# Layer 2's weight conversion in another order, with the squares' remainder put back by three points

## The chip, the cores and the metric

The kernel runs on one NeuronCore of one Trainium2 chip. The metric is the device time of one execution in microseconds (us). Before the change the median of three runs is 893.32 us (893.29 to 895.34).

Engines are named as the profile names them: PE multiplies matrices and PEld loads its weights, DVE (VectorE) and ACT (ScalarE) work element by element, POOL is GpSimd, SP issues most transfers (DMAs). Each engine takes its instructions in the order in which they were written down.

## The reference

```python
scores = scale * np.matmul(q, k.transpose(0, 1, 3, 2))      # masked local and strided, softmax, times v
...
x = np.ascontiguousarray(attn_out.transpose(0, 2, 1, 3)).reshape(B * S, H * D)
h = x @ w_in                        # layer 1: 2304 x 512 by 512 x 2048
r = np.maximum(h, 0.0)
g = r * r
x = g @ w_out                       # 2048 x 512
h = np.maximum(x @ w_in2, 0.0)      # layer 2, same shapes
return h * h @ w_out2
```

Attention over 4 batches and 8 heads gives 2304 tokens of 512 numbers. Two layers follow, each a product to 2048 columns, a ReLU, a square and a product back to 512. The weights of both layers arrive as 64-bit floating point numbers.

## The kernel before, in words

**Numbers.** Matmuls run on FP32R operands, so each 32-bit operand is split into a high part (a copy rounded to FP32R, made by ACT) and a low part (value minus high, made by DVE). A product is three matmuls: high by high, low by high, high by low.

**Steps.** Layer 1 works on five blocks of tokens: 512, 512, 512, 256, 512 wide. A step `s` is one block and 128 of the 2048 columns (256 of them in the 256-wide block). The main loop issues for step `s` first `mm1(s + 1)`, 12 matmuls of 512 columns (or 24 of 256) into a PSUM bank, and then `mm2(s)`, as many into the block's four banks `ps_y`. Steps 0 to 47 are blocks 0 to 2, steps 48 to 55 the 256-wide block, steps 56 to 71 the last block. Steps 72 to 79 are the first block of layer 2, 256 wide (`narrow`); from then on layer 2 uses seven products per 2 by 2 blocks in place of eight (`seven`), for which sums and differences of the weights are needed.

**Between mm1 and mm2** (`mm1`, lines 1012 to 1022). While weights are converted, ACT makes `r`, the ReLU of the bank (L1012), `sq`, its square (L1017), and `gh`, the rounded copy (L1018). DVE makes `gl = sq - gh` (L1022), the remainder. `mm2` reads `gh` in its first eight matmuls and `gl` in the last four. `r` and `sq` have one buffer each, `gh` and `gl` two.

**Points.** Each step has eight places between matmuls at which other work may be issued: three in `mm1`, one behind it, three in `mm2`, one behind it (`point`, L1553). Once attention has been issued, about step 46, each point adds 0.6 (`w_out`) or 0.68 (`w_in`) to a credit (`PACES`), and for each whole credit `conv2_by` issues one unit of the list `conv2`.

**The conversion of layer 2's weights** (`conv2`, L433). There are 32 pieces of 128 x 512: 16 of `w_out`, then 16 of `w_in`, taken in pairs. For a piece, `sign2` puts the sign into the lower words (DVE, L242 and L246), `range2` shifts the exponent of the upper words (ACT, L263), `whole2` joins both to 32-bit values (DVE, L268), `high2` copies the high part (ACT, L368) and `rest2` takes the low part (DVE, L375). For a pair, `sums_1` and `sums_2` make four sums and differences (DVE, L386), `high_s` their high parts (ACT, L420) and `sums_3` their low parts (DVE, L386, 128x1024). Before the change, a pair's nine units run from its signs to `sums_3`, and the next pair begins behind it.

**Transfers.** For a pair of `w_out`, `rest2` of the second piece stores 1 MB to `w_mem` (L378) and `sums_3` another 1 MB (L426), both from a fixed place in `xall` that the next pair's `high2` and `high_s` overwrite. `whole2` and `sums_3` then load a raw piece of 512 KB into the buffer that they have just read (L225). Pieces of `w_in` are loaded one per step from step 56 on. All of these stand in SP's queue.

**Ends of blocks.** In a block's last step `mm2` copies each finished bank to a tile `o` (ACT, L1067) and stores it to `y_dram` (L1069), in the last two blocks of layer 1 from ACT's own queue. The tiles are `tag="pt"`, which has two buffers, so the third copy waits until the first store has landed. In steps 60 to 69 the first rows come back as `y_in` (`load_y`, `tag="s"`, also two buffers) and are split (`split_y`, L955 and L956).

Of the kernel before, what the change touches and what calls it, by code (L numbers as in the profile page):

```python
# [9 lines left out]
F32 = mybir.dt.float32  # L10
# [4 lines left out]
ALU = mybir.AluOpType  # L15
AX = mybir.AxisListType

P = 128
# [146 lines left out]
def r32(ap):  # L165
    return ap.bitcast(F32)
# [3 lines left out]
def tile_attention_then_two_mlps(  # L170
# [259 lines left out]
            load2("out")  # L430


    conv2 = []  # L433
    for i in range(0, half2 + 2, 2):
        if i:
            conv2.append([(sums_3, i - 2)])
        if i < half2:
            conv2 += [
                [(sign2, i)],
                [(sign2, i + 1), (range2, i)],  # L440
                [(whole2, i), (range2, i + 1)],
                [(whole2, i + 1), (high2, i)],
                [(sums_1, i), (high2, i + 1)],
                [(sums_2, i)],
                [(rest2, i), (high_s, i)],
                [(rest2, i + 1)],
            ]

    def conv2_by(n):
        while n and n_conv2[0] < len(conv2):  # L450
# [526 lines left out]
    def mm1(s, point):  # L977

        if s >= len(steps):
            return  # L980
        k, f = steps[s]
        ne = tiles_of(k)
        n = TB // ne
        x_hi, x_lo = block_x(k)
        if s != 1 and n_att[0] >= att_end[-1]:
            ps = ps_a.tile([P, TB], F32, tag="a", name="ps_h")
        elif s != 1:
            ps = ps_h.tile([P, TB], F32, tag="h", name="ps_h")
        else:
            ps = ps_a.tile([P, TB], F32, tag="a", name="ps_h")  # L990
        for c in range(KC):
            for e in range(ne):
                w = ready2(f + e) if k == NB else ready(("in", 0, f + e))
                for i, (a, x) in enumerate(((0, x_hi), (0, x_lo), (1, x_hi))):

                    last = c == KC - 1 and i == 2 and e == ne - 1
                    product(
                        ps[:, e * n:(e + 1) * n],
                        lhsT=w[:, c // 2, a, c % 2 * P:(c % 2 + 1) * P] if k == NB
                        else w[:, a, c * P:(c + 1) * P],  # L1000
                        rhs=x[:, c] if k == NB else x[:, c, x_at(n):x_at(n) + n],
                        start=c == 0 and e == 0 and i == 0,
                        stop=last,
                        halves=last and k == NB - 1 and f == 0,
                    )
                    one_small()
            if c < KC - 1:
                point()
        g0 = 48 if ne > 1 and blocks[k][0] == 0 else 0
        r = gpool.tile([P, TB], F32, tag="r", name="r", bufs=1)  # L1010
        sq = gpool.tile([P, TB], F32, tag="sq", name="sq", bufs=1)
        nc.scalar.activation(out=r, in_=ps, func=AF.Relu, scale=W_BACK)  # L1012
        h = gpool.tile([P, TB + P], F32R, tag="gh", name="gh", bufs=2)[:, g0:g0 + TB]
        lo = gpool.tile([P, 3 * HALF], F32R, tag="gl", name="gl", bufs=2)[:, g0:g0 + TB]
        if 0 < n_load[0] - n_part[0] or 0 < n_conv2[0] < len(conv2):

            nc.scalar.activation(out=sq, in_=r, func=AF.Square)  # L1017
            nc.scalar.activation(out=h, in_=sq, func=AF.Copy)  # L1018
        else:
            nc.scalar.activation(out=h, in_=r, func=AF.Square)  # L1020
            nc.vector.tensor_tensor(out=sq, in0=r, in1=r, op=ALU.mult)  # L1021
        nc.vector.tensor_tensor(out=lo, in0=sq, in1=r32(h), op=ALU.subtract)  # L1022
        gh[s], gl[s] = h, lo

    def mm2(s, point):

        k, f = steps[s]
        layer, j = blocks[k]
        t0, n = BLOCKS[layer][j]
        ne = tiles_of(k)  # L1030
        ws = [ready(("out", layer, f + e)) for e in range(ne)]
        h, lo = gh.pop(s), gl.pop(s)

        if f == 0:
            ys[k] = [ps_y.tile([P, 512], F32, tag=f"y{c}", name="ps_y") for c in range(KC)]
        end = f + ne == NF

        def narrow_at(s):
            return s < len(steps) and tiles_of(steps[s][0]) > 1

        todo = []
        for c, y in enumerate(ys[k]):
            cols = slice(c * P, (c + 1) * P)
            for i, (a, gp) in enumerate(((0, h), (1, h), (0, lo))):
                for e, w in enumerate(ws):
                    g0 = e * n
                    todo.append((i, c, y[:, :n], w[:, a, cols], gp[:, g0:g0 + n]))
        if not end:

            todo.sort(key=lambda t: t[0] == 2)  # L1050
        places = [-(-len(todo) * (i + 1) // 4) - 1 for i in range(3)]
        last = {t[1]: m for m, t in enumerate(todo)}
        seen = set()
        for m, (i, c, y, lhsT, rhs) in enumerate(todo):
            product(
                y,
                lhsT=lhsT,
                rhs=rhs,
                start=f == 0 and c not in seen,
                stop=end and m == last[c],  # L1060
                halves=m == len(todo) - 1 and rhs.shape[-1] == TB and narrow_at(s + 2),
            )
            seen.add(c)
            one_small()
            if end and m == last[c]:
                t = apool.tile([P, 512], F32, tag="pt", name="o")[:, :n]
                nc.scalar.activation(out=t, in_=y, func=AF.Copy, scale=W_BACK)  # L1067
                queue = nc.scalar if j >= NB - 2 else nc.sync
                queue.dma_start(out=y_dram[:, c, t0:t0 + n], in_=t)  # L1069
            if m in places:  # L1070
                point()
# [450 lines left out]
    with tc.manual_schedule():  # L1522

        zeros = gpool.tile([P, TB], F32, tag="sq", name="zeros", bufs=1)[:, :P]
        nc.vector.memset(zeros, 0.0)
        ps = ps_h.tile([P, TB], F32, tag="h", name="ps_w")[:, :P]
        for _ in range(N_WARM):
            nc.tensor.matmul(ps, lhsT=zeros, rhs=zeros, start=True, stop=True)
        warm += [ps, zeros]
        for n in range(5):  # L1530
            if n < 3:
                load_qk()
            if n == 0:
                nc.sync.dma_start(out=cst, in_=consts)
            load_v()
        rounds = 0
        while n_att[0] < att_end[0]:
            att_to(min(n_att[0] + len(ALONE), att_end[0]))
            load_ahead(START_LOAD[rounds])
            conv_by(START_CONV[rounds])  # L1540
            rounds += 1
        def nothing():
            pass

        mm1(0, nothing)
        for s in range(len(steps)):
            k, f = steps[s]
            layer, j = blocks[k]
            n_pt = [0]
            load_ahead(4)  # L1550
            for fn, k2, c in y_at.get(s, ()):
                fn(k2, c)

            def point(s=s, layer=layer, j=j, f=f):
                n_pt[0] += 1
                at = N_PT * s + n_pt[0]
                for b, (p0, p1) in enumerate(spans):
                    if at > p0:
                        lo, hi = att_end[b], att_end[b + 1]
                        if b == 0 and at < LATE * N_PT:  # L1560
                            hi = lo + (hi - lo) * EARLY // 100
                            p1 = LATE * N_PT
                        elif b == 0:
                            lo += (hi - lo) * EARLY // 100
                            p0 = LATE * N_PT
                        att_to(min(hi, lo + -(-(hi - lo) * (at - p0) // (p1 - p0))))
                if n_part[0] < half1:
                    conv_by(1)
                elif n_att[0] >= att_end[-1] and n_conv2[0] < len(conv2):
                    if not n_load2["out"]:  # L1570
                        for _ in range(4):
                            load2("out")
                    credit[0] += PACES[conv2[n_conv2[0]][0][1] >= NF]
                    while credit[0] >= 1.0:
                        conv2_by(1)
                        credit[0] -= 1.0

            if k == NB:
                narrow(s, point)
                continue  # L1580
            if s + 1 == first_2:
                narrow_w(0)
            mm1(s + 1, point)
            point()
            mm2(s, point)
            point()
            if k == NB - 1:
                load2("in")
        seven()
# [37 lines left out]
```

## Time and profile before, and how to read it

| what | value |
|---|---|
| median of three runs | 893.32 us |
| the profiled execution's own time | 893.98 us |
| its span in the trace | 892.2 us |
| PE busy | 858.4 us, 96% |
| PEld busy | 772.6 us, 87% |
| DVE busy | 684.3 us, 77% |
| ACT busy | 528.5 us, 59% |

A trace row gives the start and length of an instruction, its engine, its line, what it writes and reads, and, in brackets, how long the engine stood idle before it and what released it. A view of waits sums these by pair of engine and releaser. A view by windows gives busy time per stretch, the granted clock of PE, the busy share of the DMA engines and their GB/s. Merged rows ("x12") are equal instructions in a row. Ends of matmuls are modelled.

### The profile page before, as it was taken

Reading aid. Unit: us, or ns where it says so; the run is one execution under the profiler, and the core shown is the slowest. Engines: PE = TensorE matmul, PEld = TensorE weight load, DVE = VectorE, ACT = ScalarE, POOL = GpSimd, SP = SyncE. Lnnn points to the kernel's source line nnn. Section 1 sums busy time; section 2 is a strip of 40 time slices with the busy share of each in tenths; the row PEclk is TensorE's granted clock in tenths of the full one; section 3 lists DMA queues with packets and bytes.
Section 4 is the critical chain, followed back from the end, with each engine's and each line's share of the span. In section 5 each row is a group of like instructions: output and inputs, shape, how many; then the busy total and the mean of one; then the engine's idle time right before and its main releaser. Section 6 shows DMA issues by size and latency. Waiting matters only on the chain. (4 is left out here: it accounts for less than half of the span.)

```text
span 892.2 us, 16045 instructions
## 1 busy us (share of the span) xinstructions
PE 858.4 (96%) x5719; PEld 772.6 (87%) x5719; DVE 684.3 (77%) x1742; ACT 528.5 (59%) x1216; POOL 17.7 (2%) x15
## 2 busy tenths in 40 slices
PE   8899999999999999998988888999999999999998
PEld 8788888888788888897866667899999999999997
DVE  5899884588867775587577767578888888888876
ACT  6977774576656664565655565455555555555542
POOL 0700000000000000000000000000000000000000
PEclk9999999999999999999999999999999999999999
DMA  8956520232322221487884365467667667766664
GB/s 275 331 190 196 186 75 26 97 90 71 87 84 73 65 64 54 164 301 291 279 290 129 118 206 192 145 201 230 194 195 259 201 189 220 255 192 198 223 190 130
DMA packets 81247, 155.21 MB, mean 174 GB/s; under 512 B 7440, under 2 KB 36240, under 8 KB 78096
## 3 DMA queue, kind: packets, MB, share of 16 engines
q1 hardware_dynamic: 80016, 152.62, 52.6%
q10 hardware_dynamic: 1152, 1.57, 0.5%
q8 instruction: 45, 0.74, 0.3%
q14 instruction: 34, 0.28, 0.1%
HBM read 127.95 MB, written 26.21 MB: 173 GB/s over the span
## 5 line engine op out<-in xcount | busy, mean ns | idle before, releaser
L969 PE MATMUL ps_h<-xall,w 128*128 128x512 f32 (+1 forms) x1153 | 247.9, 358 | 0.0
L969 PEld LDWEIGHTS ps_h<-xall,w 128*128 128x128 f32 x1153 | 185.8, 189 | 26.3
L969 PE MATMUL ps_y<-gh,w 128*128 128x512 f32 (+1 forms) x640 | 159.7, 379 | 18.5 <-ACT gh L1018 13.6
L969 PEld LDWEIGHTS ps_y<-gh,w 128*128 128x128 f32 x640 | 107.5, 189 | 40.9 <-ACT gh L1018 17.8
L1256 PE MATMUL ps_m<-xall,s 128*128 128x256 f32 x768 | 104.8, 279 | 0.6 <-DVE u L1091 0.6
L1022 DVE TENSOR_TENSOR gl<-sq,gh 128x512 fp32r<-128x512 f32 x80 | 55.3, 691 | 55.5 <-ACT gh L1018 50.5
L1256 PEld LDWEIGHTS ps_m<-xall,s 128*128 128x128 f32 x768 | 95.5, 188 | 1.8 <-DVE u L1091 1.1
L1283 PE MATMUL ps_y<-w,bh 128*128 128x256 f32 x496 | 91.8, 278 | 0.0
L969 PE MATMUL ps_y<-gl,w 128*128 128x512 f32 (+1 forms) x324 | 84.9, 373 | 0.0
L1256 PE MATMUL ps_m<-xall,w 128*128 128x256 f32 x576 | 83.3, 280 | 0.0
L1012 ACT ACTIVATE r<-ps_h 128x512 f32<-128x512 f32 x80 | 47.2, 590 | 56.6 <-PE ps_h L969 47.7
L1283 PEld LDWEIGHTS ps_y<-w,bh 128*128 128x128 f32 x496 | 75.3, 188 | 0.0
L1256 PEld LDWEIGHTS ps_m<-xall,w 128*128 128x128 f32 x576 | 74.2, 188 | 0.4 <-ACT u L1336 0.4
L1283 PE MATMUL ps_y<-w,ah 128*128 128x256 f32 x372 | 70.0, 278 | 0.0
L1283 PE MATMUL ps_y<-w,bl 128*128 128x256 f32 x248 | 68.8, 277 | 0.0
L969 PEld LDWEIGHTS ps_y<-gl,w 128*128 128x128 f32 x324 | 56.3, 190 | 10.4 <-DVE gl L1022 0.9
L1021 DVE TENSOR_TENSOR sq<-r 128x512 f32<-128x512 f32 x38 | 26.3, 691 | 48.8 <-ACT r L1012 48.8
L1091 DVE SCALAR_TENSOR_TENSOR u<-ps_m,u 128x256 f32<-128x256 f32 x96 | 40.5, 421 | 26.4 <-PE ps_m L1256 26.2
L1283 PEld LDWEIGHTS ps_y<-w,ah 128*128 128x128 f32 x372 | 56.7, 189 | 0.0
L1081 ACT ACTIVATE ah<-c 128x256 fp32r<-128x256 f32 x33 | 13.7, 417 | 71.8 <-DVE c L1265 71.7
L674 ACT ACTIVATE s<-s,m 96x128 f32<-96x128 f32 (+2 forms) x88 | 34.3, 390 | 34.2 <-DVE m L558 33.6
L263 ACT ACTIVATE raw<-raw 128x512 f32<-128x512 f32 x49 | 33.1, 676 | 32.8 <-DVE raw L246 32.4
(121 smaller groups left out, 1526.5 us busy)
## 6 DMA issues: line engine op xcount, KB each, us to landing
w<-w_mem SPq DMA_DIRECT2D x221, 256.0 KB, 2.8
raw<-moe_w_in_d SPq DMA_DIRECT2D x32, 512.0 KB, 5.5
w_mem<-xall SPq DMA_DIRECT2D x16, 1024.0 KB, 5.2
raw<-moe_w_out_d SPq DMA_DIRECT2D x24, 512.0 KB, 5.3
xall<-w_mem SPq DMA_DIRECT2D x8, 1024.0 KB, 5.1
qk<-loc_qk_d SPq DMA_DIRECT2D x12, 416.0 KB, 3.1
out_d<-o SPq DMA_DIRECT2D x17, 256.0 KB, 2.4
others<-moe_w_out_d SPq DMA_DIRECT2D x8, 512.0 KB, 6.0
```

The lines of the kernel that those rows point to most:

```text
L263: nc.scalar.activation(out=upper, in_=upper, func=AF.Copy, scale=2.0 ** (W_EXP // 8 - 112))
L674: nc.scalar.activation(out=blk, in_=blk, func=AF.Exp, scale=-1.0, bias=m[:nq, j:j + 1], accum_out=dens[i][:nq, j:j + 1],)
L969: nc.tensor.matmul(y[:, c:c + w], lhsT=lhsT, rhs=rhs[:, c:c + w], start=start and c == 0, stop=stop and c + w == n,)
L1012: nc.scalar.activation(out=r, in_=ps, func=AF.Relu, scale=W_BACK)
L1021: nc.vector.tensor_tensor(out=sq, in0=r, in1=r, op=ALU.mult)
L1022: nc.vector.tensor_tensor(out=lo, in0=sq, in1=r32(h), op=ALU.subtract)
L1081: nc.scalar.activation(out=hi, in_=src, func=AF.Copy)
L1091: nc.vector.scalar_tensor_tensor(out=dst, in0=src, scalar=sign * W_BACK, in1=to, op0=ALU.mult, op1=ALU.add)
L1256: nc.tensor.matmul(ps[:, half * HT:(half + 1) * HT], lhsT=w[:, j * P:(j + 1) * P], rhs=x[:, j], start=half == 0 and j == 0 and m == 0, sto ...
L1283: nc.tensor.matmul(banks[name][:, t * HALF:(t + 1) * HALF], lhsT=g[:, rows], rhs=w, start=first and t == 0 and m == 0, stop=end and t == 1 ...
```

## The change

The list `conv2` begins with the first pair's signs and ranges. Each pair then has its own `whole2`, `sums_1`, `sums_2`, `rest2` and `sums_3`, with the next pair's two signs and two ranges between. The remainder of the squares (L1022, now L1025) is no longer issued behind `gh`, but at the third point from there, while `conv2` has begun and not ended; `point` calls `remainders` after `conv2_by`. The tiles `o` of the last two blocks of layer 1 take `tag="s"` for odd banks and `"pt"` for even ones, so four buffers in all.

```diff
-    conv2 = []
-    for i in range(0, half2 + 2, 2):
-        if i:
-            conv2.append([(sums_3, i - 2)])
-        if i < half2:
-            conv2 += [
-                [(sign2, i)],
-                [(sign2, i + 1), (range2, i)],
-                [(whole2, i), (range2, i + 1)],
-                [(whole2, i + 1), (high2, i)],
-                [(sums_1, i), (high2, i + 1)],
-                [(sums_2, i)],
-                [(rest2, i), (high_s, i)],
-                [(rest2, i + 1)],
-            ]
+    conv2 = [[(sign2, 0)], [(sign2, 1)], [(range2, 0)], [(range2, 1)]]
+    for i in range(0, half2, 2):
+        n = i + 2 if i + 2 < half2 else None
+        conv2 += [
+            [(whole2, i)],
+            [(whole2, i + 1)],
+            [(sums_1, i), (high2, i)],
+            [(sums_2, i), (high2, i + 1)],
+            [(sign2, n)],
+            [(rest2, i), (high_s, i)],
+            [(sign2, n and n + 1), (range2, n)],
+            [(rest2, i + 1)],
+            [(sums_3, i), (range2, n and n + 1)],
+        ]
...
-        nc.vector.tensor_tensor(out=lo, in0=sq, in1=r32(h), op=ALU.subtract)
+        def remainder():
+            nc.vector.tensor_tensor(out=lo, in0=sq, in1=r32(h), op=ALU.subtract)
+        if 0 < n_conv2[0] < len(conv2):
+            behind.append([3, remainder])
+        else:
+            remainder()
...
+    def remainders(all_of_them=False):
+        for one in list(behind):
+            one[0] -= 1
+            if one[0] == 0 or all_of_them:
+                one[1]()
+                behind.remove(one)
...
-                t = apool.tile([P, 512], F32, tag="pt", name="o")[:, :n]
+                t = tile_of("s" if c % 2 and j >= NB - 2 else "pt")[:, :n]
...
-                elif n_att[0] >= att_end[-1] and n_conv2[0] < len(conv2):
+                elif n_att[0] >= att_end[-1] and (behind or n_conv2[0] < len(conv2)):
...
                     while credit[0] >= 1.0:
                         conv2_by(1)
                         credit[0] -= 1.0
+                    remainders()
```

PE's order is the same in both kernels. On DVE, in the last block of layer 1 while `w_in` is converted, the rows from one remainder (`gl`) to the next were, in the kernel before (`raw` are the 64-bit words, `s` the sums, `w` the weights' parts):

```order
1014 L1022 TENSOR_TENSOR gl<-sq,gh 128x512
1015 L242 TENSOR_SCALAR raw<-raw 128x512
1016 L246 SCALAR_TENSOR_TENSOR raw<-raw 128x512
1017 L268 SCALAR_TENSOR_TENSOR val<-raw 128x512 x2
1018 L386 TENSOR_TENSOR s<-val 128x256 x2
1019 L386 TENSOR_TENSOR s<-s,val 128x256
1020 L386 TENSOR_TENSOR s<-val,s 128x256
1021 L375 TENSOR_TENSOR w<-val,w 128x2x256
1022 L1022 TENSOR_TENSOR gl<-sq,gh 128x512
1023 L375 TENSOR_TENSOR w<-val,w 128x2x256
1024 L386 TENSOR_TENSOR s<-s 128x1024
```

and in the changed kernel, in the same block:

```order
1023 L1025 TENSOR_TENSOR gl<-sq,gh 128x512
1024 L386 TENSOR_TENSOR s<-s 128x1024
1025 L268 SCALAR_TENSOR_TENSOR val<-raw 128x512 x2
1026 L386 TENSOR_TENSOR s<-val 128x256 x2
1027 L386 TENSOR_TENSOR s<-s,val 128x256
1028 L386 TENSOR_TENSOR s<-val,s 128x256
1029 L242 TENSOR_SCALAR raw<-raw 128x512
1030 L246 SCALAR_TENSOR_TENSOR raw<-raw 128x512
1031 L1025 TENSOR_TENSOR gl<-sq,gh 128x512
1032 L375 TENSOR_TENSOR w<-val,w 128x2x256
1033 L958 TENSOR_TENSOR xall<-y_in,xall 128x256
```

A sign of the next pair now stands between a pair's sums and its first `rest2` (L375), and the remainder stands behind that sign. On ACT, in the same stretch, the rows ahead of one `r` were, before (`w` and `s` are the high parts of weights and of sums):

```order
549 L263 ACTIVATE raw<-raw 128x512 x2
550 L368 ACTIVATE w<-val 128x2x256 x2
551 L420 ACTIVATE s<-s 128x1024
552 L1012 ACTIVATE r<-ps_h 128x512
553 L1017 ACTIVATE sq<-r 128x512
554 L1018 ACTIVATE gh<-sq 128x512
```

and in the changed kernel:

```order
551 L263 ACTIVATE raw<-raw 128x512 x2
552 L1014 ACTIVATE r<-ps_h 128x512
553 L1019 ACTIVATE sq<-r 128x512
554 L1020 ACTIVATE gh<-sq 128x512
555 L368 ACTIVATE w<-val 128x2x256 x2
556 L420 ACTIVATE s<-s 128x1024
557 L957 ACTIVATE xall<-y_in 128x256
558 L263 ACTIVATE raw<-raw 128x512
559 L1014 ACTIVATE r<-ps_h 128x512
```

Ranges (L263) of one pair and high parts (L368, L420) of the same pair stood together ahead of one `r`; now an `r` stands between them.

## Rows read from the trace of the kernel before

**Rows 1.** Windows, by stage: us, busy PE, PEld, DVE, ACT, POOL, PEclk, DMA, GB/s

```profile
364.00:418.00 54.00, 52.56 (x424) 50.45 (x422) 40.22 (x75) 35.58 (x57) 0.00 (x0) 1.00 0.72 263
418.00:432.00 14.00, 10.54 (x32) 7.46 (x33) 8.46 (x15) 6.99 (x13) 0.00 (x0) 0.76 0.81 281
432.00:462.00 30.00, 28.70 (x126) 23.30 (x125) 20.95 (x37) 15.94 (x26) 0.00 (x0) 1.00 0.81 286
462.00:554.00 92.00, 76.48 (x378) 61.93 (x378) 67.50 (x120) 56.40 (x91) 0.00 (x0) 0.98 0.52 170
```

**Rows 2.** Waits of PE, DVE, ACT from 372 to 570: us, times, longest

```profile
DVE gl L1022 <- ACT gh L1018: 43.8, 23, 4.5
...
PE ps_y L969 <- ACT gh L1018: 12.9, 8, 2.0
...
PE ps_y L969 <- ACT o L1067: 4.8, 5, 1.7
...
PE ps_y L1124 <- ACT gh L1018: 3.6, 2, 1.8
```

**Rows 3.** Timeline of PE: starts of `mm1`, one row per step

```profile
369.51 2.90 PE L969 MATMUL ps_h<-xall,w 128*128 128x256 f32 x24
376.47 2.88 PE L969 MATMUL ps_h<-xall,w 128*128 128x256 f32 x24
381.91 2.88 PE L969 MATMUL ps_h<-xall,w 128*128 128x256 f32 x24
...
414.59 2.90 PE L969 MATMUL ps_h<-xall,w 128*128 128x512 f32 x12
426.87 3.49 PE L969 MATMUL ps_h<-xall,w 128*128 128x512 f32 x12
432.92 2.88 PE L969 MATMUL ps_h<-xall,w 128*128 128x512 f32 x12
...
474.88 2.88 PE L969 MATMUL ps_h<-xall,w 128*128 128x512 f32 x12
482.59 2.88 PE L969 MATMUL ps_h<-xall,w 128*128 128x512 f32 x12
...
554.08 2.90 PE L969 MATMUL ps_h<-xall,w 128*128 128x256 f32 x24
559.61 2.99 PE L969 MATMUL ps_h<-xall,w 128*128 128x256 f32 x24
```

**Rows 4.** Timeline of all engines, one pair of `w_in`: start, us, engine, operation

```profile
470.93 0.42 DVE L242 TENSOR_SCALAR raw<-raw 128x512 int32<-128x512 int32 x1
...
476.82 1.06 ACT L420 ACTIVATE s<-s 128x1024 fp32r<-128x1024 f32 x1 [0.96 <-DVE s L386]
477.78 0.58 ACT L1012 ACTIVATE r<-ps_h 128x512 f32<-128x512 f32 x1
...
479.06 0.63 ACT L1018 ACTIVATE gh<-sq 128x512 fp32r<-128x512 f32 x1
...
479.72 0.69 DVE L1022 TENSOR_TENSOR gl<-sq,gh 128x512 fp32r<-128x512 f32 x1 [2.33 <-ACT gh L1018]
479.74 2.11 PE L969 MATMUL ps_y<-gh,w 128*128 128x512 f32 x8 [1.97 <-ACT gh L1018]
480.33 0.68 DVE L375 TENSOR_TENSOR w<-val,w 128x512 fp32r<-128x512 f32 x1
...
482.06 0.42 DVE L242 TENSOR_SCALAR raw<-raw 128x512 int32<-128x512 int32 x1
```

**Rows 5.** Timeline of ACT and PE at the end of the 256-wide block

```profile
420.83 0.38 ACT L1067 ACTIVATE o<-ps_y 128x256 f32<-128x256 f32 x1 [1.84 <-DMA y_dram<-o]
...
421.27 1.22 PE L969 MATMUL ps_y<-gh,w 128*128 128x512 f32 x2 [1.49 <-ACT o L1067]
```

**Rows 6.** From issue to landing of the stores at L378

```profile
DMA to landing us min/median/max: 3.8/4.0/5.5
```

**Rows 7.** From issue to landing of the stores at L426

```profile
DMA to landing us min/median/max: 5.1/6.3/7.2
```

More of the change, by code (lines that the diff above doesn't have):

```diff
@@ L430, in sums_3 @@
             load2("out")
-    conv2 = []
-    for i in range(0, half2 + 2, 2):
-        if i:
-            conv2.append([(sums_3, i - 2)])
-        if i < half2:
-            conv2 += [
-                [(sign2, i)],
-                [(sign2, i + 1), (range2, i)],
-                [(whole2, i), (range2, i + 1)],
-                [(whole2, i + 1), (high2, i)],
-                [(sums_1, i), (high2, i + 1)],
-                [(sums_2, i)],
-                [(rest2, i), (high_s, i)],
-                [(rest2, i + 1)],
-            ]
+    conv2 = [[(sign2, 0)], [(sign2, 1)], [(range2, 0)], [(range2, 1)]]
[12 more added lines that the diff above has]
+        ]
+    conv2 = [[one for one in unit if one[1] is not None] for unit in conv2]
+    conv2 = [unit for unit in conv2 if unit]
     def conv2_by(n):
@@ L1021, in mm1 @@
             nc.vector.tensor_tensor(out=sq, in0=r, in1=r, op=ALU.mult)
-        nc.vector.tensor_tensor(out=lo, in0=sq, in1=r32(h), op=ALU.subtract)
-        gh[s], gl[s] = h, lo
+        def remainder():
[4 more added lines that the diff above has]
+            remainder()
+        gh[s], gl[s] = h, lo
+    behind = []
+    def remainders(all_of_them=False):
[4 more added lines that the diff above has]
+                behind.remove(one)
     def mm2(s, point):
@@ L1572, in point @@
                             load2("out")
-                    credit[0] += PACES[conv2[n_conv2[0]][0][1] >= NF]
+                    if n_conv2[0] < len(conv2):
+                        credit[0] += PACES[conv2[n_conv2[0]][0][1] >= NF]
                     while credit[0] >= 1.0:
```

## The prediction

> **What bounds the kernel now.** I read the windows first, to see where PE is not full. Up to 418 us and from 432 to 462 PE is busy nearly throughout. From 418 to 432 it is busy for 10.5 of 14 us, with a mean granted clock of 0.76, and from 462 to 554 for 76.5 of 92 us at 0.98 [rows 1]. So there are two places to look at: the end of the 256-wide block, and the stretch in which `w_in` is converted. DVE is busy for 67.5 of those 92 us, ACT for 56.4, so neither is full by its mean.
>
> The waits come second. PE waits for `gh` eight times (12.9 us) and twice more (3.6 us) at L1124, and five times (4.8 us) for a copy `o`. DVE waits 43.8 us for `gh` ahead of the remainder [rows 2].
>
> Waits alone make the loss too small, so third I take the distance between starts of `mm1`, one per step. An undisturbed step lasts 5.44 us (376.47 to 381.91) and 5.53 in `narrow` (554.08 to 559.61). From 369.51 to 554.08 there are 28 steps in 184.57 us, five of them in `narrow`; undisturbed they would take 23 x 5.44 + 5 x 5.53 = 152.8 us. The loss is 31.8 us [rows 3]. It holds the waits, the slower matmuls after them, and matmuls whose modelled end covers a pause. The waits of rows 2 sum to 21.3 us. The Trainium skill ("Perfetto Trace Analysis", section "Tensor Engine Instruction (MATMUL, LDWEIGHTS)") says that PE's end times are estimated and not observed. Summed by waits, the gain below would be some 20 us; I go by the starts, which need no end.
>
> Three parts of the 31.8 us can be told apart [rows 3]:
> - the end of block 2: 369.51 to 376.47 is 6.96 us, 1.5 over;
> - the end of the 256-wide block: 414.59 to 426.87 is 12.28 us, 6.8 over, and the next step (to 432.92) 0.6 over, so 7.4;
> - all the rest, 22.9 us: steps like 474.88 to 482.59, 7.71 us, 2.3 over.
>
> **Why such a step is long.** In rows 4 ACT's `r` starts at 477.78, directly behind the high part of the sums, which had waited 0.96 us for DVE. The bank for this `r` was full half a step (2.7 us) before the next `mm1` began at 474.88 [rows 3], at 472.2. From the start of `r` to the end of `gh` are 1.9 us (477.78 to 479.69), so `gh` could have been there at 474.1. PE has use for it once that next `mm1` is through, at 477.6: that leaves 3.5 us of room. Here `gh` came 5.6 us late, and PE stood. DVE meanwhile stood 2.33 us ahead of its remainder, with the rest of the pair queued behind it. So DVE waits for ACT's squares, then ACT waits for DVE's sums with the next squares queued behind: one loop, of DVE's work plus ACT's 1.9 us.
>
> **The change, part by part.**
>
> *Remainder three points later, signs and ranges a pair ahead.* No instruction is added or removed; PE's order stands. While ACT makes `r`, `sq` and `gh`, DVE can now do three points of conversion: 3/8 of a 5.44 us step, 2.0 us, against 1.9 to 2.3 us of waiting. The order shows it: a sign and sums stand ahead of the remainder, and on ACT one `r` has only the ranges, the other one pair's high parts ahead of it. What DVE must do in a step is then what counts. One pair took from 470.93 to 482.06 less 2.33 of waiting and two remainders of 0.61 (479.72 to 480.33): 7.6 us [rows 4]. At 0.68 units a point, eight points a step and nine units a pair, a step holds 0.60 pairs: 4.6 + 0.6, and 0.2 for a `split_y` in every second step (0.42 taken from the equally short first row of rows 4): 5.4 us against PE's 5.44. For `w_out` it is 0.53 pairs, 4.7 us. So DVE just keeps up, and the 3.5 us of room carry its irregular steps. Walking four steps through the new order with these lengths, I find `split_y`'s wait for ACT to cost DVE about 1.2 us once, and no `gh` later than 3 us after it could be had. Bounds: nothing gained (the loop stays, 0) to all 22.9. I take 22.9 less one lost step of 2.0, so 20.9, nearest the row of an undisturbed step, because room and excess work point that way.
>
> *Later remainder as a wait.* `gl` is read by the last four matmuls of `mm2`, a step after it is issued, and the next `sq` must wait for it, six points later, about 4 us. Both are covered by that time unless DVE falls a further 3 us behind; then PE waits as before. Cost 0 to 2, taken as 0.
>
> *Four buffers for `o`.* ACT's third copy waited 1.84 us for a landing, and PE 1.49 us behind it, and again for the fourth [rows 5]. With four tiles no copy waits for a store. What is late next is only the copies themselves, four of 0.4 us behind `gh`, in 5.44 us. So the 7.4 us go: waits, and the slow matmuls that followed them at the granted clock of 0.76, a mean of its levels 1.2 and 2.4 GHz. Bounds 1.5 (the one wait of PE in rows 5) to 7.4; I take 7.4, since an undisturbed step is what is left. The `"s"` buffers are free then: `y_in` comes in step 60 and is split by step 69.
>
> *Block 2's end.* It keeps two buffers and SP's queue. Its 1.5 us stay; bounds 0 to 1.5 gained.
>
> *SP's queue.* The same transfers stand in it. The stores of `w_out` must now land sooner: L378's is followed by the next `high2` after four units in place of five, 4.5 us at 0.6 units a point and 0.68 us a point. It lands in 4.0 us (5.5 at most) [rows 6]. L426's has six units in place of seven, 6.8 us, and lands in 6.3 (7.2 at most) [rows 7]. A late one holds ACT and the `r` behind it, inside 3.5 us of room. Taken as 0; the price otherwise is the second rival.
>
> **Sum.** 20.9 + 7.4 = 28.3 us. The profiled execution took 893.98 us itself, so 865.7; the median of the runs is 0.7 lower, so I predict **865.0 us**. About 0.3% (2.7 us) is what measuring can tell from no change.
>
> **Rivals.**
>
> 1. *DVE is the bound of the `w_in` half.* For it: 5.4 of 5.44 us leaves it no room for waits of its own. Against: 3.5 us of room before PE notices, and `range2` and `high_s` now lie units ahead of their readers. If DVE still loses 1.2 us in each of some 13 steps, steps last 6.6 us: 13 x 1.16 - 3.5 = 11.6 us lost instead of 2.0, 874.6 us. Chance 0.17.
>
> 2. *The stores pace the `w_out` half.* A loop per pair: a store lands, `high2` twice (0.6 each), then `r` to `gh` (1.9), the remainder (0.6), sign and `rest2` (1.7), a store again: 5.6 us plus the landing, against 10.2 us that PE gives a pair (15 points). At 4.0 us it does not bind, at 5.5 a pair takes 11.1: seven pairs lose 0.9 each less 3.5 of room, 2.8 us; at 7.2, the longest of rows 7, 2.6 each, 14.7 us. I put it at 4 us, 869. Against: 4.0 is the usual landing, and PE ran undisturbed steps beside these stores [rows 3]. The Trainium skill ("DMA: Bandwidth & Descriptors", section "Bandwidth") gives 6.15 us for a 1 MB transfer; by that figure, an estimate, a pair would take 11.8 us, the loss would be 7.4 us and the time 872.4. Chance 0.10.
>
> 3. *Slower: that loop with late landings.* The same place, when transfers queue up: `w_in` loads join the stores from step 56. It must lose more than the 28.3 us gained, so 31.8 with the room, 4.5 a pair: a landing over 9.1 us, every time. At 10 us it is 5.4 x 7 - 3.5 = 34.3 lost, 865.0 + 34.3 = 899 us. No store took over 7.2 [rows 7]. Chance 0.02.
>
> 4. *Only the buffers help.* The remainder comes later, yet the loop closes over another wait, and the 22.9 us stay: 893.3 - 7.4 = 886 us. Against: the order shows work put where DVE stood. Chance 0.03.
>
> **How the numbers follow.** The forecast has 0.68: its range is 861.5 (all 31.8 us) to 868 (three more short waits). Up to 873 I take in the second rival and the better half of the first; left out are the rest of the first (0.09), the third and fourth (0.05), and a few hundredths below. So 861.5 to 873. Faster: all but the third rival and a little for the unseen, 0.96; same 0.02; slower 0.02.
>
> **What would show it.** Right: starts of `mm1` 5.4 to 5.6 us apart from step 49 on, except at the end of block 2; no wait of ACT's copies for `y_dram` in the 256-wide block, and a granted clock of 1.00 there; DVE's wait ahead of the remainder a small part of 43.8 us; the 92 us of the `w_in` stretch down to some 73. Wrong: steps of 6 us and more with DVE busy nearly throughout (rival 1); ACT waiting for `w_mem` at L368 or L420 and stores landing after 5 us and more (2, 3); DVE still 2 us ahead of each remainder (4).

## The result, and the profile after

The changed kernel takes 867.33 us (median of four runs, 866.58 to 867.61). The kernel before took 893.57 beside it (893.29 to 895.34). The ratio is 0.9701 with a 95% interval of 0.9684 to 0.9718: 26.2 us faster, 2.3 us above the forecast of 865.0 and inside its range. The profiled execution took 866.58 us itself, with a span of 864.8.

The windows come first, by the same stages as [rows 1]; the last one is 24 us shorter than there, because the stretch itself became shorter.

```profile
364.00:418.00 54.00, 52.54 (x425) 50.74 (x424) 39.95 (x75) 33.67 (x55) 0.00 (x0) 1.00 0.67 245
418.00:432.00 14.00, 13.36 (x57) 10.07 (x57) 11.79 (x22) 11.15 (x19) 0.00 (x0) 1.00 0.97 356
...
462.00:530.00 68.00, 67.70 (x375) 58.87 (x374) 61.65 (x110) 48.37 (x80) 0.00 (x0) 1.00 0.65 221
```

PE (first of the busy times) is now busy for 67.7 of 68 us where `w_in` is converted. From 418 to 432 its granted clock is 1.00, the level of 2.4 GHz throughout, where before it was 0.76.

The waits from 360 to 545 answer to [rows 2] (us, times, longest us):

```profile
ACT xall L368 <- DMA w_mem<-xall: 13.5, 5, 4.0
...
DVE gl L1025 <- ACT gh L1020: 8.2, 9, 1.9
ACT xall L420 <- DMA w_mem<-xall: 7.8, 6, 2.4
DVE others L242 <- DMA others<-moe_w_out_d: 5.1, 2, 3.6
...
DVE raw L242 <- DMA raw<-moe_w_out_d: 4.5, 2, 2.6
...
ACT o L1085 <- DMA y_dram<-o: 1.7, 1, 1.7
...
PE ps_y L971 <- ACT gh L1020: 0.9, 1, 0.9
...
PE ps_y L971 <- DVE gl L1025: 0.5, 1, 0.5
PE ps_y L971 <- ACT o L1085: 0.5, 1, 0.5
...
PE ps_y L1142 <- ACT gh L1020: 0.3, 1, 0.3
```

DVE's wait ahead of the remainder fell from 43.8 to 8.2 us, PE's waits from 21.3 to 2.2. ACT now waits 21.3 us for stores of `w_mem` (13.5 + 7.8), nearly all of it without PE noticing. In the kernel before, it waited for them once:

```profile
ACT xall L420 <- DMA w_mem<-xall: 1.1, 1, 1.1
```

DVE now waits 9.6 us (5.1 + 4.5) for raw pieces of `w_out`; in the kernel before, no such wait is listed.

The starts of `mm1` answer to [rows 3]:

```profile
369.68 2.90 PE L971 MATMUL ps_h<-xall,w 128*128 128x256 f32 x24
375.14 2.88 PE L971 MATMUL ps_h<-xall,w 128*128 128x256 f32 x24
...
407.78 2.90 PE L971 MATMUL ps_h<-xall,w 128*128 128x512 f32 x13
415.27 2.90 PE L971 MATMUL ps_h<-xall,w 128*128 128x512 f32 x12
422.24 2.88 PE L971 MATMUL ps_h<-xall,w 128*128 128x512 f32 x12
...
526.66 2.90 PE L971 MATMUL ps_h<-xall,w 128*128 128x256 f32 x24
```

The 28 steps take 526.66 - 369.68 = 156.98 us, 4.2 over the undisturbed 152.8. Before it was 31.8 over, so 27.6 us were won here; the span fell by 27.4 (892.2 to 864.8). All of the gain lies in this stretch. Counted by PE's waits it would have been 19.1 us (21.3 - 2.2), so the starts were the right measure. This agrees with the sentence of the Trainium skill ("Perfetto Trace Analysis", section "Tensor Engine Instruction (MATMUL, LD_WEIGHTS)") that PE's ends are estimated. The 21.3 us of PE's waits and the 21.3 us of ACT's are equal by chance.

Most of what is left stands in two steps at the end of the 256-wide block: 7.49 us (2.05 over) and 6.97 us (1.53 over). This is the timeline of ACT, DVE, PE and SP's queue there:

```profile
404.60 1.16 ACT L368 ACTIVATE xall<-val 128x512 fp32r<-128x512 f32 x2 [1.97 <-DMA w_mem<-xall]
...
408.12 1.06 ACT L420 ACTIVATE xall<-others 128x1024 fp32r<-128x1024 f32 x1 [2.36 <-DMA w_mem<-xall]
...
409.33 0.43 DVE L242 TENSOR_SCALAR raw<-raw 128x512 int32<-128x512 int32 x1 [1.91 <-DMA raw<-moe_w_out_d]
409.65 0.57 ACT L1014 ACTIVATE r<-ps_h 128x512 f32<-128x512 f32 x1
...
410.41 0.68 DVE L375 TENSOR_TENSOR xall<-val,xall 128x512 fp32r<-128x512 f32 x1
...
411.12 0.33 SPq L378 DMA_DIRECT2D w_mem<-xall  x1
...
411.60 0.74 PE L971 MATMUL ps_y<-gh,w 128*128 128x256 f32 x4 [0.91 <-ACT gh L1020]
...
415.07 0.63 ACT L368 ACTIVATE xall<-val 128x512 fp32r<-128x512 f32 x1 [2.95 <-DMA w_mem<-xall]
...
415.61 0.58 ACT L1014 ACTIVATE r<-ps_h 128x512 f32<-128x512 f32 x1
```

ACT has stood for a store of `w_mem` before 408.12 and again before 415.07, and each time an `r` is queued behind it. The store issued at 411.12 frees ACT at 415.07, 3.95 us later. ACT had been idle since 412.12 (415.07 less 2.95), 1.0 us after the issue, where the prediction reckoned 4.5 us between the two. DVE's `rest2` (L375, 410.41), behind which this store is issued, itself stood behind a sign that had waited 1.91 us for its raw piece.

The landing times of the eight stores at L378, and then of the eight at L426, are:

```profile
DMA to landing us min/median/max: 3.9/3.9/5.1
```

```profile
DMA to landing us min/median/max: 5.6/6.3/8.0
```

The medians were 4.0 and 6.3 before [rows 6] [rows 7]. So the usual store lands no later than before; only the longest at L426 grew, from 7.2 to 8.0 us. The copy that wants the space now stands there earlier, and at 415.07 also because its store was issued late.

### The profile page after: what moved, and what is told of

It is laid out like the page before. It is cut to its first block, busy times and chain, and to the rows that moved or that the text cites. A ratio compares the mean times of both kernels' runs of the same rounds, so it can differ in the third digit from the quotient of the medians.

```text
span 864.8 us, 16060 instructions
## 1 busy us (share of the span) xinstructions
PE 851.5 (98%) x5719; PEld 771.6 (89%) x5719; DVE 683.0 (79%) x1742; ACT 526.1 (61%) x1216; POOL 17.7 (2%) x15
## 5 line engine op out<-in xcount | busy, mean ns | idle before, releaser
L971 PE MATMUL ps_y<-gh,w 128*128 128x512 f32 (+1 forms) x640 | 156.8, 375 | 2.3 <-ACT gh L1020 1.6
L1025 DVE TENSOR_TENSOR gl<-sq,gh 128x512 fp32r<-128x512 f32 x80 | 55.2, 690 | 17.6 <-ACT gh L1020 13.2
L1301 PE MATMUL ps_y<-w,al 128*128 128x256 f32 x186 | 51.6, 277 | 0.0
```

The lines of the kernel that those rows point to most:

```text
L971: nc.tensor.matmul(y[:, c:c + w], lhsT=lhsT, rhs=rhs[:, c:c + w], start=start and c == 0, stop=stop and c + w == n,)
L1301: nc.tensor.matmul(banks[name][:, t * HALF:(t + 1) * HALF], lhsT=g[:, rows], rhs=w, start=first and t == 0 and m == 0, stop=end and t == 1 ...
```

## The experiments

"Loss" is the distance between starts of `mm1` over 5.44 us a step (5.53 in `narrow`), as in the prediction, one profiled execution each. The stages run from the start of one `mm1` to that of another: A from step 49 to 55 (the end of block 2 and five steps behind it), B from 55 to 59 (with the end of the 256-wide block), C from 59 to 64 (the rest of the `w_out` half), D from 64 to 72 (the `w_in` half ahead of `narrow`), E from 72 to 77 (five `narrow` steps).

| kernel | median, us | ratio, 95% interval | A | B | C | D | E | loss, us |
|---|---|---|---|---|---|---|---|---|
| before | 893.57 | 1 | 1.5 | 7.5 | 1.7 | 12.6 | 8.5 | 31.8 |
| the change | 867.33 | 0.9701, 0.9684 to 0.9718 | 0.0 | 3.6 | 0.0 | 0.0 | 0.6 | 4.2 |
| order_alone | 889.01 | 0.9934, 0.9917 to 0.9952 | 7.2 | 10.7 | 3.0 | 1.4 | 4.2 | 26.6 |
| remainder_alone | 873.28 | 0.9760, 0.9740 to 0.9781 | 2.6 | 1.4 | 0.0 | 1.7 | 7.2 | 12.9 |
| buffers_alone | 890.51 | 0.9951, 0.9936 to 0.9965 | 1.5 | 2.1 | 4.6 | 12.5 | 8.3 | 29.0 |
| without_buffers | 876.06 | 0.9785, 0.9761 to 0.9809 | 3.8 | 6.0 | 0.0 | 0.0 | 4.1 | 14.0 |
| after_again | 866.65 | 0.9693, 0.9679 to 0.9708 | 2.1 | 2.4 | 0.0 | 0.0 | 0.7 | 5.3 |
| remainder_and_buffers | 867.77 | 0.9706, 0.9691 to 0.9720 | 1.5 | 0.1 | 0.0 | 1.0 | 3.2 | 5.8 |
| remainder_1 | 873.51 | 0.9769, 0.9755 to 0.9784 | 3.0 | 5.5 | 2.1 | 0.0 | 1.1 | 11.7 |
| remainder_6 | 864.90 | 0.9676, 0.9659 to 0.9692 | 0.0 | 0.2 | 0.4 | 0.0 | 1.4 | 2.0 |
| pace_out_55 | 864.35 | 0.9674, 0.9659 to 0.9689 | 2.1 | 0.1 | 0.1 | 0.0 | 0.0 | 2.2 |
| pace_in_85 | 871.83 | 0.9764, 0.9744 to 0.9784 | 1.6 | 2.9 | 0.0 | 4.3 | 0.8 | 9.7 |
| old_list_6 | 871.37 | 0.9750, 0.9734 to 0.9767 | 1.5 | 1.1 | 0.0 | 1.1 | 4.8 | 8.5 |
| remainder_6_pace | 866.06 | 0.9691, 0.9677 to 0.9706 | 0.0 | 0.1 | 0.0 | 0.0 | 2.1 | 2.2 |

Ratios are to the kernel before on the same chip beside them (893.39 to 895.21 us for the three groups of experiments). Where groups are compared below "by ratio", the difference of two ratios is taken of 893.57 us. The change and after_again are one program: their A differs by 2.1 us and their B by 1.1, so differences of that size in one stage show nothing by themselves. The profiled execution of remainder_alone was the slowest of its four (875.91 us), so its loss is some 2.6 us above that of its median.

### The parts of the change, each alone

**order_alone**: the new list, the remainder issued at once, two buffers.

```diff
-        if 0 < n_conv2[0] < len(conv2):
+        if False:
...
-                t = tile_of("s" if c % 2 and j >= NB - 2 else "pt")[:, :n]
+                t = apool.tile([P, 512], F32, tag="pt", name="o")[:, :n]
```

> The new list of units, the remainder again directly behind gh, two buffers for the copies o. Theory A (one loop of DVE's work and ACT's 1.9 us; it opens if DVE has work while ACT squares, or if ACT's squares stand behind nothing that DVE has just made; either half does most of it): about 873 us, 7 for the buffers and some 2 for waits left over 865. Theory B (only the later remainder opens the loop, since DVE still stands 2 us ahead of it): 886 to 893 us, with DVE's wait ahead of the remainder still near 40 us. Theory C (only the buffers matter): 893 us.

It gains 5.9 us (0.66%), within theory B's range. That is a sum of two signs. In D the loss falls from 12.6 to 1.4: with signs and ranges between the pairs, the loop in the `w_in` half is open even though the remainder stands where it stood. From A to C it rises from 10.7 to 20.9. Its waits from 362 to 560:

```profile
DVE gl L1025 <- ACT gh L1020: 45.4, 23, 5.8
ACT xall L368 <- DMA w_mem<-xall: 18.2, 5, 4.8
...
ACT o L1085 <- DMA y_dram<-o: 9.1, 3, 5.4
...
PE ps_y L971 <- ACT o L1085: 8.3, 5, 2.9
```

One place where it got worse is the end of block 2, where the step grew from 6.96 to 9.20 us:

```profile
375.05 0.60 ACT L1085 ACTIVATE o<-ps_y 128x512 f32<-128x512 f32 x1 [5.41 <-DMA y_dram<-o]
...
375.70 0.72 PE L971 MATMUL ps_y<-gh,w 128*128 128x256 f32 x4 [2.87 <-ACT o L1085]
...
379.02 0.69 DVE L1025 TENSOR_TENSOR gl<-sq,gh 128x512 fp32r<-128x512 f32 x1 [5.77 <-ACT gh L1020]
```

ACT stands 5.41 us for a store, PE behind it, and DVE 5.77 us ahead of its remainder with the conversion queued behind. With the remainder at once, an ACT that waits for a transfer holds DVE too.

**remainder_alone**: the old list, the remainder three points later, two buffers.

```diff
-    conv2 = [[(sign2, 0)], [(sign2, 1)], [(range2, 0)], [(range2, 1)]]
...
+    conv2 = []
+    for i in range(0, half2 + 2, 2):
...
-                t = tile_of("s" if c % 2 and j >= NB - 2 else "pt")[:, :n]
+                t = apool.tile([P, 512], F32, tag="pt", name="o")[:, :n]
```

> The old list of units, the remainder three points later, two buffers for o. Theory A: about 878 us: DVE works on while ACT squares, but r still stands behind the high part of sums that DVE has just made, so a part of the loop stays. Theory B: 872 to 874 us, all but the buffers' 7 us gained. Theory C: 893 us.

It gains 21.4 us (2.4%), as theory B had it, the largest part by far. Of its 12.9 us of loss one step of 12.26 us holds 6.7, at the end of the last block:

```profile
514.47 0.60 ACT L1084 ACTIVATE o<-ps_y 128x512 f32<-128x512 f32 x1 [3.94 <-DMA y_dram<-o]
...
518.12 0.58 ACT L1013 ACTIVATE r<-ps_h 128x512 f32<-128x512 f32 x1
...
520.07 3.47 PE L1141 MATMUL ps_y<-xall,gh 128*128 128x512 f32 x8 [4.83 <-ACT gh L1019]
```

The third copy waits 3.94 us for a buffer, `r` stands behind it and the conversion, and PE waits 4.83 us for `gh`. The copies of the last block want four buffers too, which the prediction had not priced.

**buffers_alone**: the old list, the remainder at once, four buffers.

```diff
-    conv2 = [[(sign2, 0)], [(sign2, 1)], [(range2, 0)], [(range2, 1)]]
...
+    conv2 = []
+    for i in range(0, half2 + 2, 2):
...
-        if 0 < n_conv2[0] < len(conv2):
+        if False:
```

> The old list, the remainder directly behind gh, four buffers for o. Theories A and B: 886 us, the 7.4 us at the end of the 256-wide block gone and nothing else; the steps after 462 us keep their 7.4 to 7.7 us. Theory C: 867 us.

It gains 4.4 us (0.5%), less than the 7 of theories A and B. B falls from 7.5 to 2.1, but C rises from 1.7 to 4.6: in steps 59 and 60 PE now waits for `gh` as well. That the long pause had let the conversion catch up there is a reading, not shown.

**without_buffers**: the change with two buffers again.

```diff
-                t = tile_of("s" if c % 2 and j >= NB - 2 else "pt")[:, :n]
+                t = apool.tile([P, 512], F32, tag="pt", name="o")[:, :n]
```

> The changed kernel with two buffers for o. Theories A and B: 872 to 874 us, one long step at the end of the 256-wide block with copies waiting for the stores to y_dram and a granted clock well below 1 there. If the other two parts make that wait harmless too (ACT is there earlier): 868 us.

By ratio it is 7.5 us slower than the change, a little more than theories A and B had; the granted clock from 414 to 428 us is 0.81. Its profiled execution is 9.8 us longer than the change's. In B and E, where the tiles act, it loses 5.9 us more. Another 3.8 us it loses in A, where the tiles can't act yet; there its timeline has

```profile
398.60 1.06 ACT L420 ACTIVATE xall<-raw 128x1024 fp32r<-128x1024 f32 x1 [3.61 <-DMA w_mem<-xall]
...
401.52 3.15 PE L971 MATMUL ps_y<-gh,w 128*128 128x256 f32 x16 [1.80 <-ACT gh L1020]
```

and the change's has, for the same copy,

```profile
396.55 1.06 ACT L420 ACTIVATE xall<-raw 128x1024 fp32r<-128x1024 f32 x1 [2.28 <-DMA w_mem<-xall]
```

A wait for a store of 2.28 us is covered there, and one of 3.61 is not: PE waits 1.80 us. The same copy waits 3.52 us in after_again, and PE 0.74. So the cover of the stores is nearly used up also away from the block's end, and losses in A differ between executions that issue the same there. The three parts alone sum to 5.9 + 21.4 + 4.4 = 31.7 us, the change gives 26.7 (its ratio on 893.57): they share the end of the 256-wide block and the loop.

**after_again** (the change itself) and **remainder_and_buffers** (the change with the old list) were measured beside each other.

```diff
-    conv2 = [[(sign2, 0)], [(sign2, 1)], [(range2, 0)], [(range2, 1)]]
...
+    conv2 = []
+    for i in range(0, half2 + 2, 2):
```

> The changed kernel itself, on the chip of the next three: all theories 867 us, as before.

> The old list of units, with the later remainder and the four buffers. Theory D (the later remainder opens the loop by itself and the buffers close two long steps; the new list adds nothing and costs waits of ACT for stores to w_mem): 864 to 867 us, no step over 6.6 us. Theory E (the new list does its part once the copies o no longer wait): 869 to 872 us, the changed kernel 2 us or more ahead.

They are 866.65 and 867.77 us, and their intervals overlap; the second lies between the forecasts of theories D and E. With the remainder three points later and four buffers, the new list is worth some 1 us and no more is shown. What it takes from D and E (4.2 to 0.7), it mostly gives back in B (0.1 to 2.4). The waits of ACT for stores in remainder_and_buffers say why:

```profile
ACT xall L368 <- DMA w_mem<-xall: 2.9, 3, 1.3
...
ACT xall L420 <- DMA w_mem<-xall: 0.5, 1, 0.5
```

That is 3.4 us, against 21.3 in the change, and DVE's waits for raw pieces are absent, as in all five profiles with the old list; all nine with the new list have them. So most of the change's waits for transfers come with the new list, which asks for each store one unit sooner and signs the next pair's raw pieces before a pair is done.

### How late the remainder should come

**remainder_1** and **remainder_6**: one point, and six, in place of three.

```diff
-            behind.append([3, remainder])
+            behind.append([1, remainder])
```

> The changed kernel with the remainder one point behind gh in place of three. Theory D, with the size of the prediction (DVE needs as much work ahead of the remainder as ACT's squares last, 1.9 us, and a point holds about 0.7): DVE still stands 1.2 us ahead of it in a step, steps of the w_in half last about 6.5 us, 876 to 882 us. If any work at all between them is enough: 867 us.

> The changed kernel with the remainder six points behind gh. Theory D: DVE's wait ahead of the remainder falls to 1 us or less in all and the time stays within 1.5 us of 867, since that wait was no longer on PE's path. If the remainder's readers decide instead (PE's last four matmuls, ACT's next square): PE waits for gl and ACT's square for DVE, 870 us and more.

With one point DVE's wait is 22.9 us and the kernel is 6.9 us slower than after_again, between the two forecasts, so the distance matters. But the loss lies in A to C (10.6 of 11.7), not in D, where it was expected. With six points the wait is down to 0.4 us, and the time is 864.90, 1.8 us under after_again. Six points cost little behind them: ACT's `sq` waits for the remainder six times, 2.6 us in all, PE itself never waits for `gl`, and E holds 1.4 us of loss in place of 0.7.

**old_list_6**: the old list, four buffers, six points.

```diff
-    conv2 = [[(sign2, 0)], [(sign2, 1)], [(range2, 0)], [(range2, 1)]]
...
+    conv2 = []
+    for i in range(0, half2 + 2, 2):
...
-            behind.append([3, remainder])
+            behind.append([6, remainder])
```

> The old list of units, four buffers, the remainder six points later. If the new list is worth 1 us at any place of the remainder: 866 us. If the remainder's place alone counts: 864.5 to 865 us, as with the new list.

This is 871.37 us, by ratio 6.6 above remainder_6 and 3.9 above remainder_and_buffers; neither forecast had it. Its waits point to the reason:

```profile
PE ps_y L1141 <- DVE gl L1024: 3.2, 3, 2.3
...
PE ps_y L970 <- DVE gl L1024: 1.5, 2, 0.8
```

PE now waits for the remainder itself, up to 2.3 us. This is the price that the prediction named for "later remainder as a wait" and took as 0. With the new list PE's wait for `gl` is 0.5 us in the change and none at six points; with the old list at six points it is 4.7. So the list, worth some 1 us at three points, is worth 6.6 at six.

### DVE's room in the `w_in` half, and the stores

**pace_in_85** converts `w_in` at 0.85 units a point in place of 0.68.

```diff
-PACES = 0.6, 0.68
+PACES = 0.6, 0.85
```

> The changed kernel with 0.85 in place of 0.68 units a point while w_in is converted: the same work in fewer steps. If DVE was nearly full there as the prediction has it (5.4 of 5.44 us a step), a step now holds 6.5 us of DVE's work for some 10.6 steps: 1.1 us too much in each, less 3.5 us of room, 8 us lost, 875 us. If DVE's work is smaller than reckoned: below 869 us.

Steps of `w_in` last 5.7 to 6.6 us, mean 6.2. The windows of this kernel, and of the change, over that stretch:

```profile
466.52:503.50 36.98, 34.90 (x147) 26.53 (x145) 36.40 (x69) 27.23 (x44) 0.00 (x0) 1.00 0.43 142
```

```profile
465.76:498.41 32.65, 32.65 (x146) 27.08 (x145) 32.14 (x59) 24.52 (x41) 0.00 (x0) 1.00 0.49 162
```

DVE (third of the busy times) is full in both, 98%. In the change PE is full beside it; with a quarter more conversion per step PE falls to 94%, and DVE sets the step. The change keeps up with nothing to spare, as the prediction's 5.4 of 5.44 us said. The forecast for this run, 6.5 us a step, was 0.3 too long, and its time, 871.83 us, lies between the two forecasts of 875 and below 869.

**pace_out_55** converts `w_out` at 0.55 units a point.

```diff
-PACES = 0.6, 0.68
+PACES = 0.55, 0.68
```

> The changed kernel with 0.55 in place of 0.6 units a point while w_out is converted, so that each store has 9% more time to land. Theory F (the two long steps left in the changed kernel, at the end of the 256-wide block, come from ACT's copies waiting for stores to w_mem and DVE's early signs waiting for raw loads): ACT's waits for w_mem fall from 21 us to below 12, the two steps shrink, 864 to 866 us. Theory G (they come from the copies o alone): the waits fall, the steps stay, 867 us.

The time is 864.35 us, by ratio 1.7 under after_again, and the two long steps are gone (B 0.1). But its waits are neither theory's:

```profile
ACT xall L368 <- DMA w_mem<-xall: 18.4, 6, 5.3
...
ACT xall L420 <- DMA w_mem<-xall: 3.3, 4, 1.8
...
DVE others L242 <- DMA others<-moe_w_out_d: 2.2, 1, 2.2
DVE raw L242 <- DMA raw<-moe_w_out_d: 2.2, 3, 1.0
```

ACT waits 21.7 us for the stores, no less than the change's 21.3. What fell is DVE's wait for raw pieces, 9.6 to 4.4 us. Whether that, or only where the waits fall beside the block's end, took the loss away is not settled.

**remainder_6_pace**: six points, and 0.56 units a point.

```diff
-PACES = 0.6, 0.68
+PACES = 0.56, 0.68
...
-            behind.append([3, remainder])
+            behind.append([6, remainder])
```

> The changed kernel with the remainder six points later and 0.56 units a point for w_out. Theory F: 863.5 to 865 us, a little under the 864.9 of six points alone, with fewer waits for w_mem. If nothing is left to gain there, or the conversion now ends too late for the steps of layer 2's first block: 865 to 867 us.

Together they give 866.06 us, no better than either alone, as the second forecast had it. ACT's waits for stores did fall, to 4.9 us, but each change alone already clears stage B. E loses 2.1 us (PE waits 1.5 us for `gl` there), and the step behind E takes 7.13 us where the change's takes 5.54. The best versions measured are pace_out_55 and remainder_6, 864.35 and 864.90 us. By ratio that is 0.2% to 0.3% under the change; the intervals overlap, though the four runs of remainder_6 (864.12 to 865.49) and of after_again beside it (866.11 to 867.39) don't overlap.

## Why the prediction was right, and where it was not

**The bound: right.** The loop "DVE waits for ACT's squares, then ACT waits for DVE's sums" was the cost, and opening it gave the gain. DVE's wait fell from 43.8 to 8.2 us, and the lengths of steps went with it. Rival 4 (only the buffers help, 886 us) is out: the buffers alone give 4.4 us.

**"All the rest", 20.9 of 22.9 us: right, a little low.** Outside the two block ends 0.6 us of loss is left, so 22.3 were gained. No step was lost to `split_y`. The `w_in` stretch (steps 64 to 77) lasts 71.8 us where some 73 were forecast; one of its steps, of 6.16 us, lies outside the 5.4 to 5.6 us that were to show it. What the prediction gave as one term is two, and either is enough in the `w_in` half up to `narrow`: the list alone leaves 1.4 us of loss in D, the later remainder alone 1.7. In the `w_out` half only the later remainder helps of the two; the list alone makes it worse by 10.2 us from A to C.

**"Four buffers for `o`", 7.4 us: mis-sized for this kernel.** No copy of the 256-wide block waits for `y_dram` any more, and the clock there is 1.00, as forecast. Yet 3.9 us were gained at that place, not 7.4 (7.49 + 6.97 us for two steps, where 5.44 each was assumed). An undisturbed step can be had there: with the old list, remainder_and_buffers has B at 0.1. But the buffers are only one way to it, since remainder_alone, with two of them, has B at 1.4. In the change the next wait in ACT's queue shows: the copies at L368 and L420, which wait for stores of `w_mem`, with `r` queued behind them. Against that, the buffers bring 3.5 us in E (4.1 in without_buffers, 0.6 in the change), which the prediction did not count.

**"The stores of `w_out`", taken as 0: the step that failed behind that.** It said that a late store is covered by 3.5 us of room. ACT waited 21.3 us in eleven waits (1.1 us in one wait before), and the room did cover all but the ones that ended at 408 and 415, where several follow each other. Nor did the sum have the 9.6 us for which DVE now stands for raw pieces; the store of 411.12 was issued late by such a wait. Both sorts of wait come with the new list. So rival 2's mechanism does occur, in the change at one place for 3.6 us, and not spread over seven pairs as it was priced; in without_buffers it struck once more, with a wait of 3.61 us. (The terms that rival 2 prints for its loop sum to 5.4 us and not to 5.6; nothing here turns on it.) The median landing didn't lengthen (3.9 us at L378 against 4.0). The Trainium skill ("DMA: Bandwidth & Descriptors", section "Bandwidth") gives 6.15 us for 1 MB, measured for loads; the stores of L378 took 3.9 us here in the median, and those of L426 took 6.3. How much of the 3.6 us is due to the stores and how much to the raw pieces is not settled, as pace_out_55 shows.

**"Block 2's end", 1.5 us stay: wrong here, and not a fixed price.** The step lasts 5.46 us in the change though its copy still waits 1.7 us for `y_dram`. It goes with the conversion work that meets it: 6.95 to 6.98 us in all five profiles with the old list, 5.46 to 5.54 in seven with the new list and a later remainder, 7.50 in pace_out_55 and 9.20 in order_alone.

**"DVE just keeps up": right.** DVE is 98% busy beside a full PE; rival 1 (DVE the bound) needs a quarter more work per step, and then it comes.

**"Three points against 1.9 to 2.3 us of waiting": right in kind.** One point loses 6.9 us and six gain 1.8; but the place was the `w_out` half, where ACT is held by stores, and not the `w_in` half from which the length had been read.

**The sum.** 865.7 forecast for the profiled execution, less 1.4 (rest) and 1.5 (block 2), plus 3.5 (the end of the 256-wide block), is 866.3; it took 866.58. The change's median is 0.75 us above its profiled execution, and that of before 0.4 below its own. The errors of the terms partly cancelled, so it is in part luck that the median came within 2.3 us of the forecast.

## What to carry to other kernels

Where two engines in order wait for each other in turn, look for an instruction that waits at the head of a queue though nobody needs its result soon, and issue it later, behind work that is ready; here this one move alone was worth 21 us of 893. Work put further ahead also asks for its transfers sooner: the new list opened the `w_in` half as well, but ACT's waits for stores went from 1.1 to 21.3 us with it, and near the 256-wide block's end they were no longer covered. So when a wait on the path is removed, look for the next wait behind it before you price its place by an undisturbed step. Measure the parts apart, since two of them may buy the same microseconds, and one (the list) may cost where another is missing.

## What the runs showed of the hardware

The same rows of matmuls, without any idle time and at a granted clock of 1.00, ran at two rates in two executions of the same program. The change's timeline of PE and then that of after_again, in the 256-wide block:

```profile
380.58 2.88 PE L971 MATMUL ps_h<-xall,w 128*128 128x256 f32 x24
...
386.02 2.88 PE L971 MATMUL ps_h<-xall,w 128*128 128x256 f32 x24
```

```profile
380.58 2.99 PE L971 MATMUL ps_h<-xall,w 128*128 128x256 f32 x24
...
386.23 2.99 PE L971 MATMUL ps_h<-xall,w 128*128 128x256 f32 x24
```

A step lasts 5.44 us in the one and 5.65 in the other, 4% more; four such steps make 0.9 of the 2.1 us that after_again loses in stage A. The cause is open, and no experiment was made on it. Losses of a microsecond in stage A are not to be read as waits.
